# Decode attention on one core: PV with V as the moving operand, and the out projection summed in rows over a layer

## The chip, the cores and the metric

The kernel runs on one core of a Trainium2 chip. The metric is device time in microseconds (us) of one execution. Shares and rows below come from one profiled execution of the kernel before; its span is the time from the first to the last instruction that the profile shows.

## What is computed

One decode step of four sequences through two layers that share their weights and their cache. A layer is a grouped-query attention over a cache of 4096 positions followed by a gated feed-forward block, each with a layer norm before it and a residual around it.

```python
B, Sq, D = 4, 1, 512            # bf16 throughout
Hq, Hkv, Sk, Dh = 32, 8, 4096, 128   # 4 query heads share one cache head
F = 1792
...
def attention(x, k_cache, v_cache, wq, wo):
    q = (x @ wq) in heads
    scores = einsum("bhqd,bhkd->bhqk", q, k) * Dh ** -0.5
    o = einsum("bhqk,bhkd->bhqd", softmax(scores), v)
    return o in rows @ wo
def feed_forward(x, w_gate, w_up, w_down):
    return einsum((sigmoid(x @ w_gate) * (x @ w_up)), w_down)
x = A_x
x = x + attention(layernorm(x), ...)
x = x + feed_forward(layernorm(x), ...)
x = x + attention(layernorm(x), ...)
x = x + feed_forward(layernorm(x), ...)
```

K and V of one cache head of one sequence are 1 MB each (4096 x 128 in bf16), 64 MB in all, and both layers read all of them.

## The kernel before

**Units and pairs.** A unit is one layer, one sequence and one cache head with its four query heads; there are 64. Two neighbouring heads make a pair, and the table ORDER gives the order of the 32 pairs as three digits (layer, sequence, pair of heads). A sequence enters layer 1 when its layer-0 pairs and its feed-forward pass are through, so pairs of both layers are mixed.

**Slots and loads.** K and V of a unit each take one of 12 slots of 1 MB in SBUF; when wq is no longer needed, its four parts become slots too. KEPT lists the heads whose K or V stays in its slot from layer 0 to layer 1 (before: 20 K and 6 V). LOADS is the order of the DMAs, all from SP's queue: k, v, o (a part of wo), g, u, d (the feed-forward weights). The function pump issues the next load as soon as the program has given a slot back; SP then waits for the last reader of that slot.

**A pair's steps.** PROGRAM is an order written out by hand, one letter for a step; every engine gets its instructions in this order and runs them in order.

- T or t: k_turn (L971), DVE transposes K in 32x32 blocks in place.
- b: q_blocks (L724), POOL copies the q of the pair from SBUF (qs) into a block pattern (qz), four copies of 32x32.
- s: scores (L988), 16 matmuls of 512 columns, in four column strips of the array (PSUM partitions 0, 32, 64, 96), four to a strip.
- m, p, n: row maxima on DVE (L1003), spread over the partitions by a matmul (L1008), and turned into a bias on DVE (L1017).
- e: the exponential on ACT with its row sum (L1028). h: the sum is split into two bf16 parts on POOL (L1058, L1061).
- P: 16 small matmuls transpose the probabilities into PSUM (L1047); C and D: eight copies of 32x128 to SBUF on ACT (L1081).
- r, i: row sums over the partitions by two matmuls (L1094), and their reciprocal on DVE (L1106).
- a: pv, once per unit (L1120). A 128x128 block of V is the stationary operand and 4 columns of probabilities move; 32 matmuls add up to the 128x4 output. Two PSUM banks, O_ps, take turns.
- o: normalise (L1159), DVE multiplies by the reciprocal. w or W: the out projection (wo_units, L1178), 32 matmuls of one or two moving columns with 128x128 blocks of wo as stationary; where two sequences of layer 1 need the same heads, they share the matmuls as two columns. DVE adds the result to x (L1194).
- a dot: the next piece of a sequence's feed-forward pass and of its next q projection (pass_steps: gate rows L790, up rows L815, down L910, q rows L861, layer norm sums L484 and L571).

**Data in PSUM.** Eight banks: two for scores, one for the transposed probabilities (PT), one for small things (MS), two for O_ps, two for the passes (M_ps). The class _Sched turns reads and writes of named keys into semaphore waits.

**The end.** After PROGRAM, row sums and PV of the last pair, whose last V comes in two halves, then the remaining out projections, a layer norm and the last feed-forward for all four sequences (L738, L1391), and the output DMA (L1410).

Of the kernel before, what the change touches and what calls it, by code (L numbers as in the profile page):

```python
# [33 lines left out]
class _Sched:  # L34

    def __init__(self):
        self.prog = {e: [] for e in ENGINES}
        self.all_items = []
        self.last_write = {}
        self.readers = {}  # L40

# [13 lines left out]
    def group(self, eng, fns, reads=(), writes=(), deps=(), sem_key=None, inc=1, needed=False):  # L55
# [6 lines left out]
        for k in writes:  # L62
            w = self.last_write.get(k)
            if w is not None:
                deps.append(w)
            deps.extend(self.readers.get(k, ()))
        tok = None
        first = True
        for fn in fns:
            tok = self._inst(eng, fn, deps if first else (), sem_key, inc, needed)  # L70
            first = False
        for k in writes:
            self.last_write[k] = tok
            self.readers[k] = []
# [4 lines left out]
    def inst(self, eng, fn, reads=(), writes=(), deps=()):  # L79
        return self.group(eng, [fn], reads=reads, writes=writes, deps=deps)  # L80
# [42 lines left out]
KEPT = ["012345/23", "0145/45", "167/67", "0134567/"]  # L123
ORDER = """
002 000 003 001 013 011 101 010 012 100 102 021 022 020 023 112 110 113 103 031 123 030 033 032 120
111 121 130 122 131 132 133
"""
LOADS = """
okkkvokkog kkovkkvvkv vvookvkogo uuddvvvkkv kkvvkkvvvv kkkvvkvvkk vvvvvvkkkv kvvkvkvkvv kvkkvkvkvv
kvvkkvkvkv kvkvkvvvvv vvvvvv  # L130
"""
PROGRAM = """
smpnehTWPbT smbDrpTiCneaTahT sPormpiDCnaebPhTTta somrpbinCDet sahmrPapCWoniwDaTabePoT
shWw.mw.CpD..r.ne.Piw.h...ra..aCDoi...a.T.bW stmtpnabWwehx sorPCmiwtpnWwDaethaPTrobx sCimDWbaapnex
sPhrompnDTbix seWwCmahPbpaTo snemWp.CWrnDWbi.aahPtotr...DT. se.Cibm.p.ha.anrw.Po.CiTe...DaTPaDhCr.
sbtmpotn.WePhiaWT sabmDpworCn siwamePpba shrneDoiwCwPmaapohnrCwiDeT.baTaP.
soCD.bm.phrn.tie.atwh.TaoP.r sim.p.WCwtDbnae...h.tatotP.r sDCmip.Wanw.aoePbtCwhr sitbmTpDanaePohwr
stDimptbCneaahPDTori sCamWpbnaehPDottCrwiaT smWapbnoeTWPChWriD sampneaobhwPrtC.it..D..T.a
s.bm...aTW.pneoW...hT.P. s.DbTwmCr sWipnaWmewTphaPrnbDC soiampenhPTbraoieCh sDrmbPpnaaoe
siCWbDamPpanhCr soimDapeaohrPDCiwanehaPoCDw  # L140
# [3 lines left out]
def bass_interleave_layers__gqa_block_cached__glu_gated_glu__decode_kernel(  # L144
# [60 lines left out]
    qs_sb = [sbt([P, NT4, HQ], dt.bfloat16, f"qs{b}") for b in range(Bn)]  # L205
    qz_sb = sbt([P, 2, NT4, 4, REP], dt.bfloat16, "qz")
    oT_sb = sbt([P, HQ, 2], dt.bfloat16, "oT")
    pe_sb = sbt([P, 4, P], dt.bfloat16, "pe")
    pT_sb = sbt([P, 2, 2, 4, 4, REP], dt.bfloat16, "pT")
    NSMALL = 128  # L210
# [25 lines left out]
    head_f = small(2 * REP)  # L236
    mask_f = small(8, 2 * REP, dtype=dt.bfloat16)
    rden_sb = small(2 * REP)
# [23 lines left out]
    half_f = t_row[:, P:P + 8 * REP].rearrange("p (u w) -> p u w", u=2)  # L262
    gs_sb = t_row[:, 0:KF * Bn]
# [4 lines left out]
    QZ = [f"qz{a}" for a in range(4)]  # L268
# [4 lines left out]
    O_ps = [pst("O_ps0"), pst("O_ps1")]  # L273
    M_ps = [pst("M_ps0"), pst("M_ps1")]

# [91 lines left out]
    def dve(fn, reads=(), writes=()):  # L367
        return S.inst("dve", fn, reads=reads, writes=writes)

    def act(fn, reads=(), writes=()):  # L370
        return S.inst("act", fn, reads=reads, writes=writes)
# [10 lines left out]

    S.inst("pool", lambda e: e.memset(qz_sb[:, :, :, :, :], 0.0), writes=QZ + ["pf"])

# [40 lines left out]
    dve(lambda e: e.memset(M_ps[1][:, :], 0.0), writes=["M1"])  # L425
    act(lambda e: e.activation(ident_f[:, :], ident_bf[:, :], ACTF.Copy), reads=IDENT, writes=["ra"])
# [3 lines left out]
    def head_masks():  # L430
# [33 lines left out]
        dve(lambda e: e.tensor_reduce(rm_sb, head_f, AX.X, ALU.add), reads=["head"], writes=["rm"])  # L464
        dve(
# [11 lines left out]
    def ln_a(b0, nb, mult, sums=None):  # L477
# [28 lines left out]
        if nb == 1:  # L506
# [3 lines left out]
                reads=["rc"] + QZ,  # L510
                writes=["xcb", "pf"],
# [94 lines left out]
    def mean_of_last(us, batches):  # L606
        u = seq[NU - 1][2]
        assert us == [u]
        for c, bb in enumerate(batches):
            if bb is not None:  # L610
                S.last_write["M1"] = S.group(
                    "pe",
                    [
                        (lambda n, r, c, bb: lambda e: e.matmul(
                            M_ps[1][:, bb:bb + 1], lhsT=ws_hl[:, n, r:r + 1].broadcast_to([P, P]),
                            rhs=oT_sb[:, u * REP + r, c:c + 1], start=False, stop=(n == 1 and r == REP - 1),
                        ))(n, r, c, bb)
                        for n in range(2) for r in range(REP)
                    ],
                    reads=["wsb", f"oT_{u}_{c}"],  # L620
                )
# [69 lines left out]
    def q_spread(b0, nb):  # L691
# [15 lines left out]
        for bi in range(nb):  # L707
            act(
                (lambda bi: lambda e: e.activation(  # L709
                    qs_sb[b0 + bi][:, :, :],  # L710
                    M_ps[1][:, 0:NT4 * N].rearrange("p (t h b) -> p t h b", t=NT4, b=nb)[:, :, :, bi],
# [3 lines left out]
                writes=[f"qs{b0 + bi}"],  # L715
            )

    def q_blocks(g):
        _, b, u = seq[2 * g]
        for a in range(4):  # L720
            ps = slice(32 * a, 32 * a + 32)
            S.inst(
                "pool",
# [738 lines left out]
```

## Time and profile before

| | us |
|---|---|
| median of three runs | 315.37 |
| lowest and highest | 315.33, 315.67 |
| the profiled execution | 316.22 |
| its span | 314.2 |
| PE busy in the span | 223.9 |
| DVE busy | 174.5 |
| ACT busy | 104.5 |
| POOL busy | 40.4 |

The kernel reads 120.85 MB from HBM. The profile gives the busy time of each engine, the span in 40 slices of 7.855 us with busy shares in tenths, groups of instructions by source line, and for an idle engine the instruction that ended its wait. PE is TensorE's matmuls and PEld its weight loads; SPq is the queue from which the loads are issued. The granted clock is the share of TensorE's clock that the profile says was granted. Ends of matmuls are modelled, so the time from the start of one group to the start of the next says more than a group's duration.

### The profile page before, as it was taken

Reading aid. Unit: us, or ns where it says so; the run is one execution under the profiler, and the core shown is the slowest. Engines: PE = TensorE matmul, PEld = TensorE weight load, DVE = VectorE, ACT = ScalarE, POOL = GpSimd, SP = SyncE. Lnnn points to the kernel's source line nnn. Section 1 sums busy time; section 2 is a strip of 40 time slices with the busy share of each in tenths; the row PEclk is TensorE's granted clock in tenths of the full one; section 3 lists DMA queues with packets and bytes.
Section 4 is the critical chain, followed back from the end, with each engine's and each line's share of the span. In section 5 each row is a group of like instructions: output and inputs, shape, how many; then the busy total and the mean of one; then the engine's idle time right before and its main releaser. Section 6 shows DMA issues by size and latency. Waiting matters only on the chain.

```text
span 314.2 us, 11318 instructions
## 1 busy us (share of the span) xinstructions
PE 223.9 (71%) x4882; PEld 148.0 (47%) x4882; DVE 174.5 (56%) x411; ACT 104.5 (33%) x347; POOL 40.4 (13%) x205
## 2 busy tenths in 40 slices
PE   1223424563789888899789698887857895989686
PEld 1221212252455464546447645365635552566575
DVE  6265657415325767585853766766554858552143
ACT  2003103332013266343335622434424303544520
POOL 0002101110000123111111111021111011121000
PEclk9999999999999999995655565555555555555555
DMA  7999999999999999999999999999998999999910
GB/s 295 410 420 396 412 413 419 417 394 395 401 417 417 392 415 403 422 421 417 420 398 395 424 419 421 416 421 417 417 421 331 391 349 422 422 420 421 408 58 3
DMA packets 20936, 121.57 MB, mean 387 GB/s; under 512 B 1940, under 2 KB 6040, under 8 KB 7704
## 3 DMA queue, kind: packets, MB, share of 16 engines
q1 hardware_dynamic: 20864, 120.86, 94.8%
q8 instruction: 38, 0.62, 0.8%
q14 instruction: 10, 0.08, 0.1%
q10 hardware_dynamic: 24, 0.01, 0.0%
HBM read 120.85 MB, written 0.00 MB: 385 GB/s over the span
## 4 chain that ended last, share of the span: by engine, by line
PE 38%; DMA 36%; DVE 14%; issue 6%; ACT 3%; SPq 1%; POOL 1%; DVEq 0%; ACTq 0%; POOLq 0%
DMA slot<-in_A_v_cache_dram 23%; PE S_ps L988 11%; PE O_ps L1120 10%; DMA slot<-in_A_k_cache_dram 9%; DVE slot L971 8%; DMA wo<-in_A_wo_dram 5%; PE O_ps L1178 4%; PE M_ps L861 2%; DVE small L1003 2%; PE PT L1047 1%; PE M_ps L910 1%; ACT pT L1081 1%; ACT pe L1028 1%; PE M_ps L815 1%; PE M_ps L484 1%
## 5 line engine op out<-in xcount | busy, mean ns | idle before, releaser
L971 DVE STREAM_TRANSPOSE slot<-slot 128x2048 f32<-128x2048 f32 (+1 forms) x54 | 98.1, 1824 | 14.6 <-DMA slot<-in_A_k_cache_dram 14.5
L1081 ACT ACTIVATE pT<-PT 32x128 bf16<-32x128 f32 x252 | 67.6, 268 | 78.1 <-PE PT L1047 42.9
L1120 PE MATMUL O_ps<-pT,slot 128*128 128x4 bf16 x1888 | 58.7, 166 | 26.2 <-DMA slot<-in_A_v_cache_dram 19.9
L1120 PEld LDWEIGHTS O_ps<-pT,slot 128*128 128x128 bf16 x1888 | 55.3, 104 | 39.1 <-DMA slot<-in_A_v_cache_dram 16.4
L988 PE MATMUL S_ps<-slot,qz 128*16 128x512 bf16 x496 | 59.5, 612 | 16.3 <-DVE slot L971 8.8
L1028 ACT ACTIVATE pe<-S_ps,small 128x512 bf16<-128x512 f32 x32 | 22.0, 687 | 66.5 <-DVE small L1017 28.7
L724 POOL COPY qz<-qs 32x32 bf16<-32x32 bf16 x128 | 26.0, 203 | 128.5 <-PE S_ps L988 79.2
L1003 DVE TENSOR_REDUCE small<-S_ps 128x1 bf16<-128x512 f32 x32 | 22.0, 687 | 32.8 <-PE S_ps L988 32.8
L988 PEld LDWEIGHTS S_ps<-slot,qz 128*16 128x16 bf16 x496 | 12.5, 109 | 36.5 <-issue 17.1
L1178 PE MATMUL O_ps<-oT,wo 128*128 128x1 bf16 (+1 forms) x736 | 23.5, 166 | 5.8 <-DMA wo<-in_A_wo_dram 3.2
L1178 PEld LDWEIGHTS O_ps<-oT,wo 128*128 128x128 bf16 x736 | 21.6, 104 | 11.1 <-issue 6.3
L1047 PE MATMUL PT<-ident_bf,pe 128*64 128x32 bf16 x512 | 19.2, 215 | 4.0 <-ACT pe L1028 3.9
L1047 PEld LDWEIGHTS PT<-ident_bf,pe 128*64 128x64 bf16 x512 | 15.8, 150 | 8.4 <-ACT pe L1028 7.0
L1194 DVE TENSOR_TENSOR small<-small,O_ps 128x4 f32<-128x4 f32 x33 | 4.4, 156 | 26.4 <-PE O_ps L1178 26.3
L1159 DVE TENSOR_TENSOR oT<-O_ps,small 128x8 bf16<-128x8 f32 (+1 forms) x33 | 5.4, 163 | 19.5 <-PE O_ps L1120 14.5
L1058 POOL CAST small<-small 128x1 bf16<-128x1 f32 x32 | 5.9, 186 | 78.7 <-ACT pe L1028 61.5
L1017 DVE CUSTOM_DVE_ANT_0 MS<-MS,small 128x64 f32<-128x64 f32 x32 | 9.0, 281 | 10.9 <-PE MS L1008 9.1
L861 PE MATMUL M_ps<-wq,small 128*1 128x512 bf16 x128 | 14.4, 613 | 0.0
L1008 PE MATMUL MS<-valid_p,small 128*128 128x64 bf16 x32 | 7.3, 229 | 8.4 <-DVE small L1003 8.2
L1008 PEld LDWEIGHTS MS<-valid_p,small 128*128 128x128 bf16 x32 | 3.5, 110 | 16.5 <-DVE small L1003 15.4
L709 ACT ACTIVATE qs<-M_ps 128x128 bf16<-128x128 f32 x8 | 1.9, 280 | 27.0 <-PE M_ps L698 27.0
L803 ACT ACTIVATE t_row<-M_ps,small 128x512 f32<-128x512 f32 x4 | 2.8, 688 | 21.0 <-PE M_ps L790 10.4
(111 smaller groups left out, 183.7 us busy)
## 6 DMA issues: line engine op xcount, KB each, us to landing
slot<-in_A_v_cache_dram SPq DMA_DIRECT2D x53, 1024.0 KB, 11.5
slot<-in_A_k_cache_dram SPq DMA_DIRECT2D x42, 1024.0 KB, 11.1
wq<-in_A_wq_dram SPq DMA_DIRECT2D x2, 2048.0 KB, 10.0
wo<-in_A_wo_dram SPq DMA_DIRECT2D x8, 512.0 KB, 14.4
wq<-in_A_v_cache_dram SPq DMA_DIRECT2D x4, 1024.0 KB, 18.4
wq<-in_A_k_cache_dram SPq DMA_DIRECT2D x2, 1024.0 KB, 10.1
wg<-in_B_w_gate_dram SPq DMA_DIRECT2D x2, 896.0 KB, 16.5
wu<-in_B_w_up_dram SPq DMA_DIRECT2D x2, 896.0 KB, 17.7
```

Of the source, the lines that this page charges most:

```text
L724: (lambda a, ps: lambda e: e.tensor_copy(qz_sb[ps, :, :, a, :], qs_sb[b][ps, :, u * REP:(u + 2) * REP].rearrange("p t (u r) -> p u t r", r ...
L861: (lambda k, st: lambda e: e.matmul(M_ps[h][32 * st:32 * st + 1, :], lhsT=xc_bf[:, k, 0:1], rhs=wv[:, k, h, :, st, :], start=(k == 0), sto ...
L971: dve(lambda e: e.transpose(kf, kf), writes=[f"s{st}"])
L988: (lambda t, b2, e_, c, r0, ul: lambda e: e.matmul(S_ps[p][r0:r0 + 4 * REP, :], lhsT=qz_sb[:, ul, t, :, :].rearrange("p a r -> p (a r)"), ...
L1003: dve(lambda e: e.tensor_reduce(rm_bf, S_ps[p][:, :], AX.X, ALU.max), reads=[f"S{p}"], writes=["rmb"])
L1008: lambda e: e.matmul(MS[:, 0:16 * REP], lhsT=rm_bf.broadcast_to([P, P]), rhs=valid_p[:, :], start=True, stop=True),
L1017: lambda e: e.tensor_tensor_reduce(MS[:, 128:128 + 16 * REP], MS[:, 0:16 * REP], mask_f.rearrange("p n w -> p (n w)"), rowk_f, BIG, ALU.ad ...
L1028: lambda e: e.activation(pe_sb.rearrange("p j m -> p (j m)"), S_ps[p][:, :], ACTF.Exp, bias=nm_sb, scale=exp_scale, accum_out=sm_sb,),
L1047: (lambda x1, j, a1, n: lambda e: e.matmul(PT[64 * a1:64 * a1 + 64, n:n + 32], lhsT=pe_sb[:, j, 64 * x1:64 * x1 + 64], rhs=valid_bf[:, :, ...
L1081: (lambda dst, frm: lambda e: e.activation(dst, frm, ACTF.Copy))(dst, frm),
L1120: (lambda n, x, c, j: lambda e: e.matmul(O_ps[p][:, ul * REP:(ul + 1) * REP], lhsT=vv[:, x * JG + c * 4 + j, :], rhs=pT_sb[:, x % 2, x // ...
L1178: (lambda c, r: lambda e: e.matmul(O_ps[p][:, 64 + 2 * c:64 + 2 * c + nb], lhsT=wo_sb[:, us[0] * REP + r, cols(c)], rhs=oT_sb[:, us[0] * R ...
```

## The change

**PV.** For 31 of the 32 pairs the probabilities become the stationary operand and V moves: a matmul takes 512 columns of V, that is four blocks of 128 positions side by side, against a stationary of 32 columns, and its output is one 32-partition strip of the single bank O_ps. Per unit there are eight such matmuls in two parts (letters a a), per pair 16, four to a strip. Of the four 128-column blocks of a strip's rows only one belongs to each row. own_columns (X) picks it: an ACT copy with a 0/1 scale of the first block, then three DVE operations that multiply a block by a 0/1 column and add. add_rows (l) is one fp32 matmul with the 128x128 result as stationary and a 128x8 selection as moving operand; it adds the strips up and gives the 128x8 output in the form that the kernel before had. The last pair keeps the old PV, now named pv_columns.

**Out projection.** normalise writes each head's column into a zero-padded tile oz. wo_rows (w) uses one column of it (layer 0) or four with the other sequences' columns zero (layer 1) as stationary, and 512 columns of wo move: 8 matmuls per pair, alternating between two column strips (partitions 0 and 32 in layer 0, 64 and 96 in layer 1) of a bank AC. The sums stay in AC: for a sequence in layer 0, for all four sequences in layer 1. Then rows_out copies 64 partitions of AC to SBUF on ACT, and rows_added adds the strips by four small fp32 matmuls and a DVE add to x. In layer 0 these are the first two pieces of each sequence's pass; in layer 1 they stand once, at the end, ahead of the last pair's PV. The last pair's own projection keeps the old form.

**q.** The spread q stays in PSUM (banks MS and PT) instead of SBUF, and q_blocks is one DVE multiply of 128x128 with a 0/1 mask instead of four POOL copies.

**Banks and order.** With several things in one bank, each instruction marked with a bank waits for the last instruction of every other engine on that bank. Scores are two steps of eight matmuls (s and z). KEPT, ORDER, LOADS and PROGRAM are new: 18 K and 6 V are kept, and the list of loads has 46 k instead of 44, and as many of the others.

```diff
+        use = self.bank_use.setdefault(bank, {})
+        if bank is not None:
+            deps.extend(t for e, t in use.items() if e != eng)
...
-KEPT = ["012345/23", "0145/45", "167/67", "0134567/"]
+KEPT = ["012345/15", "01/0123", "237/", "1234567/"]
 ORDER = """
-002 000 003 001 013 011 101 010 012 100 102 021 022 020 023 112 110 113 103 031 123 030 033 032 120
-111 121 130 122 131 132 133
+001 002 003 000 013 012 011 010 102 100 101 022 023 020 021 110 111 112 033 032 030 031 121 123 113
+122 120 103 130 131 132 133
 """
 LOADS = """
-okkkvokkog kkovkkvvkv vvookvkogo uuddvvvkkv kkvvkkvvvv kkkvvkvvkk vvvvvvkkkv kvvkvkvkvv kvkkvkvkvv
-kvvkkvkvkv kvkvkvvvvv vvvvvv
+kkokkoookg ovkokvvkvk vukvookvkv kgukddvkvk vvvvvvvkkv kvvkkkvvvk kvvvkkvvkk kkkkvvkvkv kvkvvvkvvk
+kvvkvvkvkv kvkkvkvvvv vvvvvvvv
 """
 PROGRAM = """
...
+szbonerwhPlmCDpaTaaina sXzbermowiPCDTlowhaTa.p s.nzaamePCD..rXT..hlpain.e.ra.boaTa.P.
+szCwXhiDm.rpan.alo.aaieTT.P.hb.wXD s.zmCpneaTl.arobaaTP shizXClDmwpobnwreTaPhaaaX szibC
+slmrDapzaanbaeomPDXph sizwCaanebalao smPpXzrCDhlnamiwoaaepranPiwXChDerlaowaiahaPXloDCw
...
+    O_ps = pst("O_ps")
+    AC = pst("AC")
+    qs_ps = [MS[:, 128 * b:128 * b + 128] for b in (1, 2, 3)] + [PT[:, 256:384]]
+    XO = [MS[:, 64 + 32 * p:96 + 32 * p] for p in range(2)]
...
     def q_blocks(g):
+        dve(
+            lambda e: e.tensor_tensor(
+                qz_sb.rearrange("p u t a r -> p (u t) a r"),
+                qs_ps[b][:, u * w:(u + 2) * w].rearrange("p (n r) -> p n r", r=REP)
+                .unsqueeze(2).broadcast_to([P, 2 * NT4, 4, REP]),
+                own_a.unsqueeze(1).unsqueeze(3).broadcast_to([P, 2 * NT4, 4, REP]),
+                ALU.mult,
+            ),
...
     def pass_steps(b0):
         return [
+            lambda: (rows_out(0), left.add(b0)),
+            lambda: rows_added(0, b0, 1),
...
+    def pv(i, part):
+        for n in range(2):
+            x = 2 * n + part
+            for c in range(2):
+                g = 2 * ul + c
+                q = 2 * n + c
+                    (lambda x, c, q, z: lambda e: e.matmul(
+                        O_ps[32 * q:32 * q + 32, :],
+                        lhsT=z,
+                        rhs=slot[s][:, (x * JG + c * 4) * DH:(x * JG + c * 4 + 4) * DH],
+                        start=first,
+                        stop=(ul == 1 and part == 1),
+                    ))(x, c, q, z[:, ZW * g - 4 * REP * ul:ZW * (g + 1) - 4 * REP * ul])
...
+    def own_columns(g):
+        act(
+            lambda e: e.activation(acc_sb[:, :], O_ps[:, 0:P], ACTF.Copy, scale=own_j[:, 0:1]),
+        for j in range(1, 4):
+            dve(
+                (lambda j: lambda e: e.scalar_tensor_tensor(
+                    out=acc_sb[:, :], in0=O_ps[:, j * P:(j + 1) * P], scalar=own_j[:, j:j + 1], in1=acc_sb[:, :],
+                    op0=ALU.mult, op1=ALU.add,
+                ))(j),
...
+    def add_rows(g):
+            lambda e: e.matmul(XO[p][:, 0:2 * REP], lhsT=acc_sb[:, :], rhs=sel_o, start=True, stop=True),
...
+    def wo_rows(g):
+        c, n = (0, 1) if l == 0 else (b, Bn)
+        for i in range(2 * REP):
+            q = 64 * l + 32 * (i % 2)
+                (lambda i, q: lambda e: e.matmul(
+                    AC[q:q + n, :],
+                    lhsT=oz_sb[:, NROW * (i + 1) - 1 - c:NROW * (i + 1) - 1 - c + n],
+                    rhs=wo_sb[:, u * REP + i, :],
...
+    def rows_out(l):
+        act(
+            lambda e: e.activation(t_row[64 * l:64 * l + 64, :], AC[64 * l:64 * l + 64, :], ACTF.Copy),
...
+    def rows_added(l, b0, nb):
+                (lambda k: lambda e: e.matmul(
+                    M_ps[1][:, 64 + k * nb:64 + (k + 1) * nb],
+                    lhsT=t_row[64 * l:64 * l + 64, cols(k)],
+                    rhs=sel_x[64 * l:64 * l + 64, 0:nb],
...
     g = NP - 1
     row_sums(g)
     row_inv(g)
+    rows_out(1)
+    rows_added(1, 0, Bn)
-    pv(2 * g)
+    pv_columns(2 * g)
     normalise(g, (0,))
-    while do_wo((g + 1) % 2, True):
-        pass
+    wo_columns(0)
```

## The prediction

> **What bounds the kernel now.** I read the page from the top, then three stretches of the run, the groups by form, PE's own timeline, the granted clock in windows of 3.41 us, and last the issues of the DMA queue.
>
> ```profile
> span 314.2 us, 11318 instructions
> PE 223.9 (71%) x4882; PEld 148.0 (47%) x4882; DVE 174.5 (56%) x411; ACT 104.5 (33%) x347; POOL 40.4 (13%) x205
> ...
> PE   1223424563789888899789698887857895989686
> DMA  7999999999999999999999999999998999999910
> ...
> q1 hardware_dynamic: 20864, 120.86, 94.8%
> ```
>
> The DMA engines are full from the first microseconds to about 300 us. PE is loose up to 80 us and dense after that. So two things lie close together: bytes, and PE's work in the later stage. The stretch from 80 to 300 us as one row (columns: length, then PE, PEld, DVE, ACT, POOL busy, granted clock, DMA share, GB/s):
>
> ```profile
> 80.00:300.00 220.00, 182.58 (x3875) 118.44 (x3877) 128.14 (x306) 85.20 (x282) 33.22 (x166) 0.66 1.00 407
> ```
>
> PE has 37.4 us left in it. That the two are coupled shows on the DMA queue: a load is issued when PE has freed its slot, and where PE was busy with a feed-forward pass no load was issued for 8 us, after which one slice of the page fell to 331 GB/s.
>
> ```profile
> 242.85 0.38 SPq L364 DMA_DIRECT2D slot<-in_A_v_cache_dram  x1
> 250.85 0.33 SPq L364 DMA_DIRECT2D slot<-in_A_k_cache_dram  x1
> ```
>
> The time: the profiled execution took 316.22 us, 2.0 more than its span of 314.2; the median shown is 315.37. I work in spans and add 1.17 at the end.
>
> **What PE's rows cost.** Groups (busy, mean ns of one | idle before), then PE's timeline (start, duration):
>
> ```profile
> L1120 PE MATMUL O_ps<-pT,slot 128*128 128x4 bf16 x1888 | 58.7, 166 | 26.2 <-DMA slot<-in_A_v_cache_dram 19.9 <-ACT pT L1081 2.3 <-DVE small L1017 2.3
> L988 PE MATMUL S_ps<-slot,qz 128*16 128x512 bf16 x496 | 59.5, 612 | 16.3 <-DVE slot L971 8.8 <-POOL qz L724 3.3 <-DVE small L641 1.6
> L484 PE MATMUL M_ps<-small 128*128 128x4 f32 x16 | 4.7, 363 | 1.5 <-DVE small L1194 0.7 <-DVE small L925 0.6
> L1401 DVE SCALAR_TENSOR_TENSOR wq<-S_ps,small,wq 128x128 bf16<-128x128 f32 x1 | 0.4, 351 | 1.9 <-PE S_ps L1391 1.9
> ```
>
> ```profile
> 126.78 1.02 PE L1120 MATMUL O_ps<-pT,slot 128*128 128x4 bf16 x32 [0.71 <-DMA slot<-in_A_v_cache_dram]
> 127.73 1.89 PE L988 MATMUL S_ps<-slot,qz 128*16 128x512 bf16 x16
> 129.54 1.01 PE L1178 MATMUL O_ps<-oT,wo 128*128 128x1 bf16 x32
> ...
> 139.05 1.08 PE L988 MATMUL S_ps<-slot,qz 128*16 128x512 bf16 x16 [0.42 <-DVE slot L971]
> ```
>
> From start to start, 32 matmuls with 4 moving columns take 0.95 us (30 ns each), and the 16 scores matmuls of 512 columns take 1.81. Those 16 stand in four column strips, four to a strip, so a round of up to four strips costs 0.45 us. That a round costs this whatever its width is an inference: the gate rows, whose last strip is half as wide, also take 1.80 us for four rounds.
>
> **The change on PE, per pair (31 of the 32 pairs of units; the last keeps the old form).**
> - PV: 64 matmuls, 2 x 0.95 = 1.90 us, become 16 of 512 columns in four strips, 4 rounds, 1.80. Gain 0.1.
> - Adding the strips: one fp32 matmul with a 128x128 stationary. L484 and its like take 0.59 us from first to last (2 records each), about 0.5 to the next start. Cost 0.5.
> - Out projection: 23 groups of 0.95 in the kernel before (736 matmuls / 32), 0.7 per pair. After: 8 matmuls of 512 columns in only two strips, so 4 rounds, 1.80. Bounds: 0.9, if a half-filled round cost half, and 1.8; the gate rows are nearest, so 1.8. Cost 1.1.
>
> Sum +1.5 us per pair. Four pairs have their PV before 80 us (8 units in the windows up to there; V arrives at the same megabytes in both load lists, within 3 MB), so 27 pairs come after: 41 us. Each of the four passes gets rows_added, 4 fp32 matmuls with a 128-column stationary, 4 x 0.5 = 2.0: 8 us. PE's work in the stretch becomes 182.6 + 49 = 232 us, of 220 there are. Some 3 us can be moved ahead (scores done early): 229.
>
> *The clock.* The granted clock says 1.00 up to 142 us without telling anything: the scores take 1.89 us in it as well as later at 0.50. After 142 us it moves in windows of 3.41 us. Columns: PE busy, granted clock, DMA.
>
> ```profile
> 135.25:138.67 3.42, 3.38 (x32) 1.00 1.03 422
> 138.67:142.08 3.41, 2.67 (x75) 1.00 0.99 416
> 142.08:145.49 3.41, 2.85 (x78) 0.50 1.01 416
> ...
> 247.88:251.30 3.42, 3.42 (x57) 0.50 1.01 419
> 251.30:254.71 3.41, 3.06 (x74) 0.50 0.91 324
> ```
>
> The scores at 139.05 ran in 1.08 us instead of 1.89: this is a truly faster window. It follows one filled with 512-column matmuls. The other two fast windows (from 148.91 and 186.45) follow windows with 2.82 and 3.17 us of such matmuls (the same windows asked for the lines L988, L790, L815 and L861 alone); 2.79 us, in the window from 247.88, was not enough. So beyond some 82% of a window the next one is fast, and all three were given up after one window, in which at most 1.1 us of such matmuls ran. I wrote PE's new order out, letter by letter of the program with the costs above: 265 us, of which 198 (75%) are 512-column matmuls, and a third of its stretches of 3.41 us lie above 83%, were PE never to wait. A fast window takes in 1.6 times the work, so it saves 2 us. With waits I count one in eight of 64 windows: 8 x 2 = 16 us. Bounds: 0, and half of all the 512-column work, some 85.
>
> *Waits.* Of the 37.4 us idle, about 8 were waits for loads, the rest for DVE, ACT and POOL in between. A PE that is late finds most of them over; I keep 15 (bounds 5 and 30). New ones are in it: PV of a pair waits until ACT and three DVE operations have read the single O_ps; add_rows waits for DVE, where a k transpose of 2.30 us can stand ahead; and three steps on PE (maximum, row sums, add_rows) now wait for DVE's last use of bank MS. PE goes in order, so scores and PV stand behind each of these waits, and the slots that they free.
>
> Sum for the stretch: 229 - 16 + 15 = 228 us, +8 against 220.
>
> **The other edits.**
> - Bytes: the list has 46 k loads instead of 44 (kept in SBUF: 18 k and 6 v instead of 20 and 6), +2.1 MB. At 415 GB/s, 2.5 us each: +5.0 us on the DMA side. Already held by PE's +8, as PE frees the slots; it is the floor if PE is fast. The two added transposes (4.6 us) are on DVE.
> - DVE: 3 x 0.35 per pair (L1401: a 128x128 from PSUM) = 33 us; q blocks 32 x 0.25 (like the 128x128 multiply of L681) = 8; transposes 4.6. From 174.5 to about 218, 69% of the span: hidden, but for the waits above.
> - ACT: 31 x 0.28 (a 128x128 copy, L709) + 5 x 0.69 = 12 us on 104.5: hidden.
> - POOL: the 128 qz copies (26 us) go. PE and PEld waited 7 us in all for them; the DVE multiply that takes their place waits in DVE's order. Nothing.
> - The tail: before, 1.55 us lie between PV of the last pair but one and the last pair's PV (300.0 to 301.55). Now own_columns 1.5, add 0.6, normalise 0.2, rows 1.8, ACT copy 0.7, rows_added 2.0 and semaphores make 7. The last pair's V comes up to 5 us later than that pair's, which hides part. Bounds 0 and +5.4; I take the middle, +2.8.
>
> Span 314.2 + 8 + 2.8 = 325; with 1.17, **326 us**.
>
> One rule of the Trainium skill speaks against the change: by "TensorEngine Tiling (Array Packing)", section Available Configurations, a change of tiling mode drains TensorE. The trace shows no such price, as L1178 (full array) started at 129.54, before the scores in strips had ended at 129.62. By that section three more switches per pair would add, as an estimate with the 166 ns that one matmul takes to pass (L1120), 31 x 0.5 = 16 us; such drains would count to rival 2.
>
> **Rivals.**
> 1. *The forecast*: PE just over its capacity, clock fast now and then; 318 to 331. Chance 0.50. For it: 229 of 220 us, and the 8 us without issues at 242.85.
> 2. *PE alone is the bound, the clock hardly moves*: with waits between the strips' short chains no window fills beyond 82%. Then 229 + 25 = 254, +34, and 314.2 + 34 + 2.8 + 1.2 = 352 at worst; with four or five fast windows 342. 331 to 352. Chance 0.24. For it: only three such windows in the trace after 135 us.
> 3. *Faster: the fast clock holds*. PV, scores and out projection are three neighbours of 1.8 us, so windows fill, and a fast window of a late PE is still filled to about two thirds (2.7 of 4.1 us per pair), against 32% in those given up. It decides from about half the windows at 1.00: PE's 229 fall below 180 us, it never delays a slot, and the DMA's lost 5 us (slices at 331, 349) and PE's backlog of the last 15 us return 4 to 5 more than the two loads take: 310 to 314.5, about 312. Chance 0.17. Against it: fast windows were given up with PE busy 2.67 and 3.28 of 3.41 us. The Trainium skill's "TensorE: Matmul & The Clock Gate", Part 1, has the clock fall back only after an idle window; by that rule it would hold here. The trace disagrees.
> 4. *Even*: a fast clock in part, the two loads paid by the recovered 5 us: 315 to 318. Chance 0.09, of which 0.03 within 0.2%, 0.06 slower.
>
> **How the numbers follow.** Slower 0.50 + 0.24 + 0.06 = 0.80, same 0.03, faster 0.17. 0.2% (0.6 us) is about what a measurement of this kernel can tell from no change. For the range I leave out some 0.08 of the lowest and 0.1 of the highest: 312 to 342.
>
> **What would show it.** PE's busy tenths near 9 from 80 us on and DMA slices under 400 GB/s there (forecast); out-projection groups of 1.8 us for 8 matmuls at 0.50, 0.9 at 1.00; mean clock after 142 us about 0.55 (forecast) or over 0.75 (rival 3); 122.95 MB read; a wait of PE on DVE at add_rows. I am wrong if a round of two strips costs less than 0.45, or if the clock holds.

## The result and the profile after

The changed kernel takes **1.0665 times** the time of the kernel before, interval 1.061 to 1.0719: about 336.5 us against 315.52 (315.33 to 315.83) on the same chip. Of its four runs (335.57, 337.48, 343.46 and 347.89 us) the two longest showed a lower granted clock (0.765 and 0.743 against 0.811 and 0.807) and are left out of the ratio, and such runs out of the medians below. 326.0 was forecast, 312 to 342 as the range.

The page of the changed kernel, with the lines that answer to those shown of before:

```profile
span 333.7 us, 7577 instructions
...
PE 221.9 (66%) x3040; PEld 104.0 (31%) x3040; DVE 213.4 (64%) x513; ACT 117.5 (35%) x383; POOL 14.7 (4%) x78
...
PE   1332052567794886965965987796666886788876
...
DMA  8999999999999899999999999988899999999900
GB/s 301 417 398 387 403 423 417 410 378 424 407 392 368 329 389 423 375 362 363 366 390 391 412 422 419 335 314 330 304 367 422 421 405 420 422 418 423 411 30 5
...
q1 hardware_dynamic: 21152, 122.96, 92.6%
```

The span is 19.5 us longer, yet PE is no busier than before (221.9 against 223.9) and has lost its nines. DVE, at 64%, isn't full either. The loads now run under 400 GB/s in 15 of the 28 slices from the eleventh (83 us) to their end, where the kernel before had six in the same slices (from 79 us). The stretch from 80 to 300 us as one row, same columns as before:

```profile
80.00:300.00 220.00, 166.18 (x2113) 74.26 (x2113) 153.65 (x360) 87.65 (x285) 10.91 (x56) 0.77 0.97 384
```

PE is busy 16.4 us less in it and idle 53.8 us instead of 37.4, at a granted clock of 0.77 instead of 0.66. The gain in clock is larger than that: before, the first 62 us of the row read 1.00 while the scores took as long as at 0.50, and in the stretch from 142 to 300 us (first row before, second row now) the clock is 0.52 against 0.77:

```profile
142.00:300.00 158.00, 129.92 (x2829) 85.24 (x2827) 92.50 (x215) 62.43 (x208) 23.36 (x117) 0.52 1.00 406
142.00:300.00 158.00, 117.67 (x1513) 51.79 (x1513) 115.94 (x263) 60.50 (x197) 7.62 (x39) 0.77 0.97 383
```

The 15.6 us of PE work that are missing come later: after 300 us there are 26.0 us of it, against 10.4 before.

So both surprises show. The clock was far better than forecast, and PE waited far more. What PE waited for, in the view of waits for that stretch (us in total, times, longest):

```profile
PE O_ps L1188 <- DMA slot<-in_A_v_cache_dram: 16.8, 14, 3.0
PE MS L1074 <- DVE qz L781: 5.1, 3, 2.7
PE MS L1224 <- DVE acc L1212: 3.4, 4, 1.8
PE S_ps L1051 <- DVE qz L781: 3.1, 2, 2.2
```

The largest is a wait for V, the others are waits behind DVE. Read alone this says "late loads" first. But SP issues a load when PE has freed its slot (138.7 us of SP's waiting stand under O_ps L1188), so a late load can be the effect of a late PE as well as its cause. A trace can't settle that; the experiments do.

### The profile page after: what moved, and what is told of

Same layout as the page of the kernel before. It is cut to its first block, busy times and chain, and to the rows that moved or that the text cites. A ratio compares the mean times of both kernels' runs of the same rounds, so it can differ in the third digit from the quotient of the medians.

```text
span 333.7 us, 7577 instructions
## 1 busy us (share of the span) xinstructions
PE 221.9 (66%) x3040; PEld 104.0 (31%) x3040; DVE 213.4 (64%) x513; ACT 117.5 (35%) x383; POOL 14.7 (4%) x78
## 5 line engine op out<-in xcount | busy, mean ns | idle before, releaser
L1188 PE MATMUL O_ps<-slot,pT 128*32 128x512 bf16 x448 | 52.8, 477 | 22.5 <-DMA slot<-in_A_v_cache_dram 16.8
L1051 PE MATMUL S_ps<-slot,qz 128*16 128x512 bf16 x504 | 48.1, 483 | 17.5 <-issue 7.7
L1212 DVE SCALAR_TENSOR_TENSOR acc<-O_ps,small,acc 128x128 f32<-128x128 f32 x93 | 32.5, 349 | 26.6 <-ACT acc L1206 22.1
L1283 PE MATMUL AC<-wo,oz 128*1 128x512 bf16 (+1 forms) x248 | 41.2, 465 | 2.6 <-DVE oz L1264 2.6
L1206 ACT ACTIVATE acc<-O_ps,small 128x128 f32<-128x128 f32 x31 | 11.3, 365 | 40.6 <-PE O_ps L1188 40.4
L1188 PEld LDWEIGHTS O_ps<-slot,pT 128*32 128x32 bf16 x448 | 12.1, 103 | 39.8 <-DMA slot<-in_A_v_cache_dram 16.9
L1224 PE MATMUL MS<-small,acc 128*128 128x8 f32 x62 | 14.3, 303 | 14.6 <-DVE acc L1212 11.2
L1074 PE MATMUL MS<-valid_p,small 128*128 128x64 bf16 x32 | 6.8, 212 | 20.7 <-DVE small L1069 12.5
L1224 PEld LDWEIGHTS MS<-small,acc 128*128 128x128 f32 x62 | 11.5, 232 | 27.4 <-DVE acc L1212 17.3
L1114 PEld LDWEIGHTS PT<-ident_bf,pe 128*64 128x64 bf16 x512 | 12.5, 126 | 14.4 <-issue 8.1
L1283 PEld LDWEIGHTS AC<-wo,oz 128*1 128x1 bf16 (+1 forms) x248 | 10.4, 93 | 19.1 <-issue 8.4
L1264 DVE TENSOR_TENSOR oz<-MS,small 128x8 bf16<-128x8 f32 (+1 forms) x33 | 5.6, 168 | 15.0 <-PE MS L1224 7.6
```

Of the source, the lines that this page charges most:

```text
L1051: (lambda t, b2, e_, c, r0, ul: lambda e: e.matmul(S_ps[p][r0:r0 + 4 * REP, :], lhsT=qz_sb[:, ul, t, :, :].rearrange("p a r -> p (a r)"), ...
L1114: (lambda x1, j, a1: lambda e: e.matmul(PT[64 * a1:64 * a1 + 64, 0:256] .rearrange("p (a x g j h) -> p x j a g h", a=2, x=2, g=4, j=4)[:, ...
L1188: (lambda x, c, q, z: lambda e: e.matmul(O_ps[32 * q:32 * q + 32, :], lhsT=z, rhs=slot[s][:, (x * JG + c * 4) * DH:(x * JG + c * 4 + 4) * DH],
L1206: lambda e: e.activation(acc_sb[:, :], O_ps[:, 0:P], ACTF.Copy, scale=own_j[:, 0:1]),
L1212: (lambda j: lambda e: e.scalar_tensor_tensor(out=acc_sb[:, :], in0=O_ps[:, j * P:(j + 1) * P], scalar=own_j[:, j:j + 1], in1=acc_sb[:, :] ...
L1224: lambda e: e.matmul(XO[p][:, 0:2 * REP], lhsT=acc_sb[:, :], rhs=sel_o, start=True, stop=True),
```

## The experiments

Three theories were open. **DVE**: the picks of own_columns, and the queue in which they stand, hold PE up. **Strips**: the two half-filled strips of the new out projection cost PE what the forecast feared. **Loads**: the new ORDER, KEPT and LOADS issue loads late, whatever the engines do. Times are medians, and a ratio with an interval compares with the kernel before on the same chip (314.8 to 316.3 us in all of them).

**One part left out or put back.**

Without the picks, in own_columns:

```diff
-        for j in range(1, 4):
+        for j in ():
```

> The changed kernel with own_columns cut to its first copy: the three DVE operations that pick blocks 2 to 4 are left out (so three quarters of the PV output is missing). DVE loses 32.5 us of work; PE's work, the loads and the order stay. Theory A (DVE stands ahead of PE: its queue of picks, k transposes and q blocks delays add_rows, the maxima and the scores, PE frees slots late, and the loads starve): 318 to 325 us, DMA slices between 100 and 260 us back over 400 GB/s. Theory B (the two added loads and the new order by themselves): 332 us or more. Theory C (the out projection in strips makes PE late): 332 us or more.

Measured: 335.87 us, ratio 1.0652 [1.0592, 1.0712]: no gain. DVE fell from 213.4 to 184.8 us and PE's waits for the picks went, but in the stage

```profile
80.00:300.00 220.00, 172.79 (x2109) 75.90 (x2109) 131.35 (x288) 86.80 (x282) 10.99 (x56) 0.72 0.96 378
```

the loads move no more than before the edit (378 GB/s). The picks alone don't explain the loss.

The old PV in every pair, in the body of pv; own_columns and add_rows do nothing:

```diff
-                        O_ps[32 * q:32 * q + 32, :],
-                        lhsT=z,
-                        rhs=slot[s][:, (x * JG + c * 4) * DH:(x * JG + c * 4 + 4) * DH],
+                            XO[p][:, ul * REP:(ul + 1) * REP],
+                            lhsT=vv[:, x * JG + c * 4 + j, :],
+                            rhs=pT_sb[:, x % 2, x // 2, 2 * ul + c, j * REP:(j + 1) * REP],
```

> The changed kernel with PV as it was before (32 matmuls of 4 columns per unit, V stationary) in all pairs, without own_columns and add_rows; out projection in rows, q in PSUM, order and loads as in the changed kernel. Theory A: 317 to 325 us, as DVE loses the same 32.5 us and PE the add, although the clock is granted less. Theory B: 330 us or more. Theory C: 332 us or more, above the changed kernel if the fast clock is lost (each group of 8 out-projection matmuls back at 1.8 us).

Measured: 355.89 us, 1.1298 [1.1241, 1.1356], some 19 us slower than the changed kernel. PE is busy 257.5 us, at a clock of 0.62 in the stage.

The out projection in columns again, pair by pair, without the sums in AC:

```diff
-                    AC[q:q + n, :],
-                    lhsT=oz_sb[:, NROW * (i + 1) - 1 - c:NROW * (i + 1) - 1 - c + n],
-                    rhs=wo_sb[:, u * REP + i, :],
+                        XO[p][:, 16 + c:17 + c],
+                        lhsT=wo_sb[:, u * REP + r, cols(c)],
+                        rhs=o_col(r),
```

> The changed kernel with the out projection as 32 matmuls of one column per pair and a DVE add to x after each pair, without the row sums in PSUM, rows_out and rows_added. Theory C: 320 to 328 us. Theory A: 333 us or more, as DVE keeps its picks and gains 5 us of adds; PE groups of 0.95 us in place of 0.9 (fast clock) to 1.8 us. The tail should shorten by 2 to 4 us in any case, since rows_out and rows_added stood ahead of the last pair's PV.

Measured: 353.4 us, 1.1208 [1.1157, 1.1259], clock 0.60 in the stage. The strips theory falls. With either 512-column form taken back the clock in the stage falls from 0.77 to about 0.6 and the time grows by 17 to 19 us. Not all of that need be the clock: the old forms write into bank MS here and wait for its other users, and the projection in columns adds DVE operations (539 instead of 513).

The kernel before with two K heads loaded again instead of kept:

```diff
-KEPT = ["012345/23", "0145/45", "167/67", "0134567/"]
+KEPT = ["012345/23", "0145/45", "167/67", "34567/"]
```

> The kernel before with two K of sequence 3 no longer kept but loaded and transposed again: 2.1 MB more, two transposes of 2.3 us more, nothing else. Bytes alone, worked out in the prediction: +5.0 us, 320.5. Theory B wants more, 325 or over; theories A and C take +3 to +6.

Measured: 319.08 us, 1.0114 [1.0071, 1.0157]: 2.1 MB and two transposes cost 3.6 us (5.0 was the forecast's figure for the bytes).

**Parts and order apart.** The changed kernel's functions with ORDER, KEPT and LOADS of before, and before's PROGRAM with the new steps put in at the old steps' places:

> All parts of the changed kernel (PV with V moving, own_columns, add_rows, out projection in rows, q in PSUM, bank waits), but with ORDER, KEPT and LOADS of the kernel before, and its PROGRAM carried over letter by letter (own_columns right after PV, add_rows, normalise and wo_rows some steps later). 120.85 MB. After the first four runs theories A and C have fallen as they stood: neither the picks nor the strips of the out projection explain the time, and putting back the old parts in the new order made it slower. Theory B now: the new order, with its loads and its kept heads, leaves too few slots in circulation (14 of its heads are kept after the eighth pair, against 10), and this costs the time: 312 to 322 us here. Theory D: the parts together (waits on the shared bank MS and on the single O_ps, DVE's longer queue) cost it in any order: 330 us or more.

Measured: 413.9 us, 1.3155 [1.3068, 1.3241]. And the old functions with the new order, carried over the same way (the projections still held back stand ahead of the last pair):

> All parts of the kernel before, with ORDER, KEPT and LOADS of the changed one and its PROGRAM carried over letter by letter (without the letters that the old parts don't have; row sums and their reciprocal ahead of PV, the old out projections forced where wo_rows stood). 122.95 MB. Theory B: 335 to 360 us, as slow as or slower than the changed kernel. Theory D: 318 to 326 us, the bytes and little else.

Measured: 342.13 us, 1.0845 [1.0787, 1.0904]; PE 223.3 us busy, loads 379 GB/s in the stage. An order written out by hand is fitted to its parts. A carried-over order is worse than a written one, so neither number is "the price of the order"; but the changed kernel without its new parts still has slow loads.

**Loads taken out.** Each load into a slot that has been filled once brings a quarter of its bytes (the rest of the slot is stale data):

```diff
+            if s in seen:
+                parts = [(d[:, 0:NJ * DH // 4], f[:, 0:NJ * DH // 4], m, y) for d, f, m, y in parts]
+            seen.add(s)
```

> The changed kernel, order, slots, waits and all engine work as they are, but each K or V load into a slot that has been filled once brings only a quarter of its bytes; the rest of the slot keeps older data. So loads cost nearly nothing, and the time left is that of the engines and their waits on each other. Theory B (too few slots in circulation, loads issued late): 280 to 305 us, well below the full kernel. Theory D (the engines' chains are the bound in any case): 322 us or more.

> The same for the kernel before. PE's busy time of 224 us and its waits on DVE, ACT and POOL (some 29 us between 80 and 300) bound it: 265 to 290 us by both theories. Its distance to the changed kernel with light loads is what the engines' work and chains cost without the loads.

Measured: 328.63 and 298.79 us. With loads out of the way the changed kernel is still 30 us behind. That is its engines' own bound, 8 us under its time with full loads. Its waits behind DVE in the stretch from 80 to 300 us, and the same kind in the kernel before with light loads:

```profile
PE S_ps L1055 <- DVE slot L1038: 6.7, 8, 1.7
PE MS L1228 <- DVE acc L1216: 4.5, 5, 1.8
PE MS L1078 <- DVE small L1073: 3.3, 4, 1.7
PE MS L1078 <- DVE qz L785: 3.2, 3, 1.9
```

```profile
PE MS L1012 <- DVE small L1007: 4.7, 8, 0.8
PE S_ps L992 <- DVE slot L975: 1.8, 6, 0.5
```

The scores wait longer for transposed K (6.7 against 1.8 us), and the waits for the picks and the q blocks are new. The spread of the maxima (L1078 here, L1012 there) waits up to 1.9 us instead of 0.8. In the first 80 us it waits another 11.0 us here.

**Slots.** The changed kernel with two V heads fewer kept (by a count through ORDER and KEPT, heads kept between their layers then hold at most 12 slots instead of 14):

```diff
-KEPT = ["012345/15", "01/0123", "237/", "1234567/"]
+KEPT = ["012345/15", "01/23", "237/", "1234567/"]
```

> The changed kernel with V of heads 0 and 1 of sequence 1 no longer kept but loaded again, 2.1 MB more; kept heads at the peak after the eighth pair 12 in place of 14. Theory B: the two loads cost about 4 us, and more than that returns where 12 slots were full: same to 5 us faster, DMA slices between 100 and 130 us over 400 GB/s. Theory D: 3 to 6 us slower.

Measured: 335.67 us once and 341.79 to 342.5 us three times. That lies across the changed kernel's own spread: inconclusive. The kernel before with one slot less:

```diff
-    free = list(range(NSLOT))
+    free = list(range(1, NSLOT))
```

> The kernel before with one of its 12 slots left unused. Between the fifth and the twenty-fifth pair kept heads hold 6.4 slots on average before and 7.5 after the change, so this gives the kernel before about the changed one's slots in circulation (4.6 and 4.5). Theory B: 325 to 335 us. Theory D: 316 to 320 us.

Measured: 325.02 us, 1.0281 [1.0232, 1.0329]. One slot is worth 9 us there.

**Both bounds at once.** The changed kernel without picks and with light loads, and the old parts in the new order with light loads:

> Light loads (a quarter of the bytes into slots filled once) and own_columns cut to its first copy, both together: three of four column blocks are left out, and most of each slot keeps older data. With light loads alone the changed kernel took 328.6 us, with the picks alone left out 336.5. Theory E, formed on those: two bounds lie one on the other, the engines' waits behind DVE (328.6 without loads) and the loads that the new order issues late for want of free slots (336.5 without the picks). Then taking both away gives 300 to 315 us. Theory D (the chains are long whatever DVE does: single O_ps, shared bank, in-order PE): 322 us or more.

> The old parts in the new order (342.1 us) with light loads. If the new order costs time through its slots and loads alone, this comes near the kernel before with light loads (298.8): 298 to 312 us. If the order makes the engines wait on each other by itself, 320 us or more.

Measured: 305.04 us (a second run took 309.96) and 319.65. Here the picks are worth 24 us (19 by the second run), after being worth nothing with full loads. The old parts in the carried-over order are 21 us slower than in their own even with light loads.

**DVE's queue emptied.** The next kernels leave out all transposes of K (104 us of DVE; the scores are taken from K as it lies):

```diff
-        dve(lambda e: e.transpose(kf, kf), writes=[f"s{st}"])
```

With light loads, the changed kernel and the kernel before; then the changed kernel with full loads:

> The changed kernel with quarter loads, and with all transposes of K left out (104 us of DVE; scores are taken from K as it lies, so the sums are others). 328.6 us with them. If PE stands behind DVE's order, of which a transpose of 2.3 us is the longest single piece, the time falls by more than 15 us: 295 to 312, and the waits of PE on MS and S_ps after DVE shrink to less than half. If the round trips themselves (bank MS, the single O_ps) hold PE whatever is queued on DVE: 318 to 328.

> The kernel before with quarter loads and without the transposes of K. 298.8 us with them. PE's own work is the bound there (220.7 of 297 us busy, loose only in the first 80), so little goes: 285 to 297 us by that. If DVE's order holds PE there as much as in the changed kernel, it falls by as many us as the changed kernel does.

> The changed kernel with its full loads and without the transposes of K (the picks stand). If there are two bounds, DVE's order and late loads, this takes away the first alone, as leaving out the picks did: 328 to 338 us, near the 336.5 without picks, and the stretch from 80 to 300 us stays below 390 GB/s. If there is one bound, DVE's order, it falls to the level of the light kernel without transposes plus little: under 322 us.

Measured: 300.36 us (28 less than with transposes), 285.55 (13 less), and 338.34, ratio 1.0718 [1.0664, 1.0771], no gain at all. DVE's queue as such is thus a large part of the engines' bound in the changed kernel. The waits themselves came out otherwise than expected, though. PE's waits on MS behind DVE, in the stage, hardly shrank (about 16 to 15 us, summed over their rows); those of the scores for DVE went (9 to 1 us). And half of the gain is in PE's busy time, not in its idle time: PE is busy 214.5 us instead of 229.6 for the same 3040 matmuls, at a granted clock of 0.81 instead of 0.75 in the stage. Without the picks it is the same: of 24 us, 18 are PE's busy time (211.9), at 0.83. So a good part of what a wait costs here seems to be the clock that PE loses with it. The kernel before shows no such thing (220.7 busy with transposes, 218.7 without). With full loads, taking 104 us off DVE changes nothing, and PE's busy time doesn't fall either (229.3).

**The loads' side, alone.** Without picks and with fewer kept; then without picks and without transposes, so that DVE has 84 us of work in all, with the kept heads as they are and with fewer:

> The changed kernel without the three DVE picks of own_columns (their columns are left out of the sums), and with two V heads of sequence 1 loaded again instead of kept: at most 12 slots are held at any point instead of 14, and there are two loads more. Without the picks the loads are the later bound (336.5 us with the kept heads as they were). If that comes from slots out of circulation, the time falls although 2.1 MB more are read: 326 to 333 us. If it comes from the order of the loads and of the readers, the two loads are paid in full: 338 to 343 us. Between 333 and 338 it tells nothing.

> The changed kernel with its full loads, without the three picks and without the transposes of K (both left out of the sums). Each alone left the time where it was (336.5, 338.3). If the loads' side is a bound of its own, both together leave it too: 328 to 338 us, although DVE then has some 85 us of work in all. If the picks and the transposes were each enough to hold the loads back, it falls under 322 us.

> The same, with two V heads of sequence 1 loaded again instead of kept (at most 12 slots held instead of 14, 2.1 MB more to read, which cost the kernel before 3.8 us). With DVE nearly empty the loads alone bind. If slots out of circulation hold the loads back, it is at least 4 us faster than the kernel beside it that keeps them; if the order of readers and loads does, it is 2 to 6 us slower.

Measured: 334.04 us, 1.0596 [1.0555, 1.0637]; 331.82, 1.0559 [1.0502, 1.0615]; 333.82, 1.0604 [1.0566, 1.0642]. With DVE nearly empty the loads alone hold the kernel at 332 us, and PE now waits for them. Its waits in the stage without picks and transposes:

```profile
PE O_ps L1187 <- DMA slot<-in_A_v_cache_dram: 22.9, 12, 4.1
PE O_ps L1187 <- issue: 6.2, 3, 3.4
PE O_ps L1187 <- ACT pT L1148: 5.5, 10, 1.5
PE O_ps L1187 <- DMA wq<-in_A_v_cache_dram: 4.3, 1, 4.3
PE MS L1073 <- DVE qz L781: 2.1, 2, 1.4
```

Fewer kept heads give no clear answer. Without the picks they took 334.04 us against 335.87, inside the range that was said to tell nothing. Without picks and transposes they took 2.0 us longer, where at least 4 us less was expected if held slots were the cause. SP's queue shows a long gap. The changed kernel, the one without picks and transposes, and the kernel before:

```profile
84.16 1.41 SPq L381 DMA_DIRECT2D slot<-in_A_k_cache_dram  x1
97.17 0.33 SPq L381 DMA_DIRECT2D slot<-in_A_v_cache_dram  x1
```

```profile
84.27 1.45 SPq L381 DMA_DIRECT2D slot<-in_A_k_cache_dram  x1
97.66 0.33 SPq L381 DMA_DIRECT2D slot<-in_A_v_cache_dram  x1
```

```profile
82.30 0.57 SPq L364 DMA_DIRECT2D slot<-in_A_k_cache_dram  x1
...
94.25 0.33 SPq L364 DMA_DIRECT2D slot<-in_A_k_cache_dram  x1
```

In all three no load is issued for 11 to 12 us. PE's timeline of the changed kernel says what it did meanwhile:

```profile
84.72 1.87 PE L1283 MATMUL AC<-wo,oz 128*1 128x512 bf16 x8 [0.51 <-DVE oz L1264]
...
87.28 1.86 PE L1304 MATMUL M_ps<-small,t_row 64*128 64x1 f32 x8 [0.52 <-ACT t_row L1295]
...
91.24 1.02 PE L851 MATMUL M_ps<-wg,small 128*1 128x512 bf16 x8
...
92.33 1.02 PE L851 MATMUL M_ps<-wg,small 128*1 128x512 bf16 x8
93.28 0.61 PE L1114 MATMUL PT<-ident_bf,pe 128*64 128x32 bf16 x16
93.82 1.55 PE L876 MATMUL M_ps<-wu,small 128*1 128x512 bf16 x16
95.33 0.63 PE L1051 MATMUL S_ps<-slot,qz 128*16 128x512 bf16 x8
```

A last projection, rows_added, the layer norm and the gate and up rows of a pass: from 84 to 95 us no scores and no PV, so no slot comes back. The kernel before is in a pass there too, so the gap by itself is not what the change brought. But the kernel before comes out of it well supplied: between 105 and 110 us, and from there to 115, it moves 387 and 411 GB/s, the changed kernel 306 and 320. A second gap of the changed kernel, of 10.7 us, begins at 198.9, again in a pass (9.5 us without picks, 10.6 without transposes, 8.0 without both). After its first gap the kernel before has none over 7.6 us.

What differs shows in how many loads are issued ahead. The next table is worked out from the traces: what was issued and not yet moved, as a mean from 80 to 270 us; the share of that time in which at most one load (1.05 MB) was left; and the DMA time lost, which is how far those 28 slices of the page stay below 421 GB/s.

| kernel | MB ahead | at most one load | DMA time lost, us |
|---|---|---|---|
| before | 2.8 | 4% | 6.6 |
| before, two K heads loaded again | 3.2 | 2% | 4.5 |
| before, 11 slots | 2.1 | 14% | 17.2 |
| changed | 2.1 | 15% | 19.7 |
| changed, no picks | 2.1 | 17% | 22.6 |
| changed, no picks, fewer kept | 2.9 | 12% | 12.5 |
| changed, neither picks nor transposes | 2.2 | 15% | 20.0 |

The changed kernel stands where the kernel before stands with one slot less, so heads held in slots are a likely part of the loads' bound. That they are all of it is not shown. A later PE lowers the first number as well (1.8 MB with the old PV put back), so the table says how far the loads ran dry and not by itself why.

**What is settled.** Two bounds lie on each other. In us, with a dash where no kernel ran:

| kernel | full loads | quarter loads |
|---|---|---|
| before | 315.5 | 298.8 |
| before, no transposes | - | 285.6 |
| changed | 336.5 | 328.6 |
| changed, no picks | 335.9 | 305.0 |
| changed, no transposes | 338.3 | 300.4 |
| changed, neither | 331.8 | - |
| old parts, new order | 342.1 | 319.7 |

Down the column of full loads nothing that lightens DVE moves the changed kernel by more than 5 us. Down the other column each such edit takes 24 or 28 us. The loads' bound is 332, the engines' 329, and only an edit of both gets below 320. The loads' bound adds up on the page: the changed kernel loses 13.1 us more of DMA time than the kernel before. These, the 5.0 forecast for the bytes and 1.5 of the tail (worked out below) make 19.6; the span grew by 19.5.

Open stays how the 13 us divide between slots held by kept heads and the order in which readers give slots back, since no other order was written and tried, and what the round trips through bank MS cost (separate banks were not tried, as PSUM is full). None of the versions that compute the whole result beat the kernel before.

## Why the prediction missed

The direction was right, the size was not: +21 instead of +10.8. By its steps:

- **"With waits I count one in eight of 64 windows: 8 x 2 = 16 us"** failed. The trace grants 0.50 or 1.00, so by the mean of 0.77, 54% of the stretch ran at 1.00. PE's work of the stage, forecast at 229 us, was done in 166.2 there and 15.6 later, 181.8: the clock saved 47 us, not 16. The forecast took its windows from a kernel whose gaps are filled with 4-column matmuls, and read "given up after one window" off them. The changed kernel's clock in such windows (columns: PE busy, granted clock, DMA share, GB/s):

```profile
91.50:94.90 3.40, 3.40 (x47) 0.50 1.07 414
94.90:98.30 3.40, 3.07 (x75) 1.00 0.96 395
98.30:101.70 3.40, 2.74 (x56) 1.00 0.92 373
101.70:105.20 3.50, 1.92 (x29) 1.00 1.01 421
105.20:108.60 3.40, 1.13 (x30) 1.00 0.82 289
108.60:112.00 3.40, 3.36 (x34) 0.50 0.69 284
...
265.59:269.00 3.41, 2.79 (x88) 1.00 1.01 408
269.00:272.41 3.41, 3.41 (x27) 0.50 1.01 399
```

  It held through a window with PE busy 1.92 of 3.50 us and fell after one with 1.13, but it also fell after one with 2.79. The prediction set the idle rule of the Trainium skill ("TensorE: Matmul & The Clock Gate", Part 1: the clock falls back after an idle window) aside because the kernel before disagreed with it. This trace disagrees too: ahead of all ten falls between 80 and 300 us PE was busy for 1.1 to 2.8 of 3.41 us, so no window was idle. What decides when the clock falls stays open.
- **"I keep 15 (bounds 5 and 30)"** of waits is the step that decided. PE was idle 53.8 us in the stretch. By the prediction's own sum, 229 - 47 + 54 = 236, not 228, against 220 there are: 8 us more than forecast, which is most of the miss. Two errors of 31 and 39 us nearly cancelled. "A PE that is late finds most of them over" was the false reason: it holds while PE is the last to be ready. Here PE, made faster by the clock, had to wait for loads and for DVE's results: 16.8 us of the stretch for V alone.
- **The order was priced by its bytes alone**, and these were "already held by PE's +8". The +5.0 for two loads is near the measured 3.6. But with the new order and its kept heads fewer loads are issued ahead (2.1 MB instead of 2.8), and the DMA engines lose 13.1 us more. No term of the sum has that. The prediction had the mechanism in its hand, as it quoted a gap of before (8 us, at 242.85) and the slow slice behind it.
- **DVE "hidden, but for the waits above"**: 218 us were forecast and 213.4 came. Hidden it is, but only behind the late loads. With the loads light, the picks were worth 24 us and the transposes 28. An engine at 64% can bind when another must pass through its queue once or twice per pair.
- **PE's prices** held. Eight matmuls of the out projection take 1.87 us at 0.50 (1.80 to the next start), and 1.03 at 1.00 (0.96 to the next start); add_rows 0.59 and 0.39; rows_added 1.86. A half-filled round does cost a full one.
- **ACT and POOL** came out as worked out: 117.5 against 104.5 + 12, and POOL's 26 us gone at no gain.
- **The tail** grew less than the +2.8 forecast, within its bounds. The last loads fade 18 us later than before (DMA share 0.49 from 317 to 318 us, before 0.46 from 299 to 300), and the span is 19.5 us longer, so 1.5 us are the tail's.
- **The drain at a change of tiling mode** (the Trainium skill, "TensorEngine Tiling (Array Packing)", Key Properties; the prediction names the section above it) was read wrongly: "the trace shows no such price". Ends of matmuls are modelled, so an overlap of 0.08 us proves nothing; the starts do show a price. In PE's timeline of the changed kernel, at a clock of 1.00:

```profile
208.60 0.64 PE L1051 MATMUL S_ps<-slot,qz 128*16 128x512 bf16 x8
209.06 0.40 PE L1188 MATMUL O_ps<-slot,pT 128*32 128x512 bf16 x4
209.39 0.26 PE L901 MATMUL M_ps<-ident_bf,t_row 128*128 128x4 bf16 x4
...
209.85 0.65 PE L1051 MATMUL S_ps<-slot,qz 128*16 128x512 bf16 x8
210.31 0.62 PE L1188 MATMUL O_ps<-slot,pT 128*32 128x512 bf16 x8
210.85 0.43 PE L1114 MATMUL PT<-ident_bf,pe 128*64 128x32 bf16 x16
```

  Eight matmuls in strips take 0.46 us to the next start when strips follow, 0.54 when another form does; four take 0.33, where half of 0.46 is 0.23. So a change out of the strips costs some 0.1 us, less than the 0.17 of the prediction's estimate, and the trace agrees with the page that a change has a price. The prediction's 1.80 us for four rounds before a full-array group has it in already (1.68 before a group in strips).
- **The rivals.** Rival 2 gave the right time (331 to 352) for the wrong reason: its clock "hardly moves". Rival 3 had the right clock ("about half the windows at 1.00") and the wrong end: "PE's 229 fall below 180 us, it never delays a slot". PE's work did fall to 182, and slots still came late, because PE itself had to wait, for DVE and for V. No rival joined a fast clock with long waits.

## What to carry to other kernels

Where a load is issued only when an engine gives a buffer back, count how many loads stay issued ahead, and give a smaller number a term of its own beside the bytes. Before a gap is named as a cause, look for the same gap in the kernel before. When taking one suspect away changes nothing, take it away once more with the other suspect's cost removed: two bounds of nearly the same height hide each other, and here each was worth over 20 us once the other was gone. An estimate for waits taken from an engine that was the bound doesn't hold once that engine gets faster.

## What was not expected of the hardware

- **Short waits cost more than their length.** With light loads, leaving out DVE work that PE waited for took 18 and 15 us off PE's busy time for the same matmuls, as the clock in the stage rose from 0.75 to 0.83 and 0.81.
- **One buffer of 1 MB is worth 9 us.** The kernel before went from 316.3 to 325.0 us with 11 instead of 12 slots, with all its instructions unchanged.
